# A unit's score maxima turned by VectorE's block transpose instead of a TensorE transpose, with sixteen row transfers in place of four

## The chip, the cores and the metric

The kernel runs on one core of one Trainium2 chip. Its time is the device time of one execution in microseconds (us); less is better.

## What is computed

The inputs are `x` (2048 x 640), attention weights `wqkv` and `wo` with 32 heads of 20 columns, four DFT matrices and a gate vector. Cut to what matters:

```python
def _A_ref(x, wqkv, wo):
    # q, k, v: 32 heads of 20 columns
    scores = jnp.einsum("bhqd,bhkd->bhqk", q, k) * (Dh ** -0.5)
    p = _softmax(scores, axis=-1)
    o = jnp.einsum("bhqk,bhkd->bhqd", p, v)
    return o @ wo
def _B_ref(x, ...):
    a, b = x @ dft_hid_re.T, x @ dft_hid_im.T
    return dft_seq_re @ a - dft_seq_im @ b
g = _sigmoid((x * gate_w).sum(-1, keepdims=True))
return g * a + (1 - g) * b
```

The softmax subtracts each query's maximum over all 2048 keys. That maximum, and the way it gets to where it is subtracted, is all that the change touches.

## The kernel before

**Units and the two score streams.** The attention is cut into 32 units (`NU`). A unit is a pair of heads (h = 0 on partitions 0 to 63, h = 1 on 64 to 127) and one half of the queries, 1024 of them. The scores are computed twice. In the first pass, "m" (`s_mm`, line 168), TensorE multiplies queries by keys with the queries on the partitions, and VectorE takes the maximum of each 128 x 512 block (line 170). In the second pass, "e" (in `score`, line 830), TensorE multiplies with the keys on the partitions and ScalarE takes the exponential (line 832). The exponential can't subtract a per-query number there, because the queries run along the free axis. So the subtraction is done in the matmul itself: `kst` has rows of ones and `qst` has two more rows per head, `KROWS` and `KROWS + 1`, which hold the negated maximum split in two parts (the second is what the first, rounded to fp32r, leaves over). The e matmul contracts over 62 rows, the m matmul over the first 60.

**How the maxima travel.** When a unit's 128 maxima tiles are done, `max_nm` (line 184) reduces them to a 128 x 16 tile of negated maxima: partition p and column 8h + q hold the query 128q + p of head h. `max_chain` (line 199) turns this by a TensorE transpose against an identity into a 16 x 128 tile in PSUM (line 202), and VectorE splits it into `m1` and `m2` (`split`, lines 112 and 113). Then SyncE copies, for each head and part, eight partitions of 128 numbers into one row of `qst` (lines 210 and 211): four transfers a unit, each in eight pieces of 512 bytes. An e matmul of the unit can start once they have landed.

**The order.** The body is one list of 256 cycles, written by hand; a unit takes eight of them:

```python
ORDER = "emFemFFFFemFeFFmeFFemFFFmmFFmeeB"
```

Each "e" and "m" is one score matmul, an "F" is a place where matmuls of the Fourier part are filled in (lines 346 and 575, later the output projection, line 646), and "B" is a burst: `max_nm` if a unit's maxima are complete, the reads of finished Fourier tiles (lines 354/355, 594/595, 655 to 658), the sixteen products of probabilities and values (`av_step`, line 494), and last `max_chain`. The m stream runs `LEAD` = 41 steps (a step is the two heads' scores of one block) ahead of the e stream. With these numbers, unit n's last m matmul stands in cycle 8n - 3, its `max_chain` at the end of that cycle's burst, and its first e matmul is the first of the two "e" at the end of cycle 8n - 1, two cycles later. `FIRST` makes that one the head h = 1. Unit 0 is handled in the prologue.

**Queues.** Every engine works through its own list in order. SyncE (SP) issues nearly all transfers: loads of DFT blocks (`raw<-in_cdft`, line 459), of operands kept in memory (`araw<-a_scr`, line 474), of partial sums (`yt<-y_scr`, line 567), of reciprocals of the softmax sums (`rb<-r_scr`, line 521), and stores (lines 679, 785). The four row transfers are put into SP's list at the second step after `max_chain`. The program gives SP's transfers eight completion semaphores in turn, so a transfer is issued only when the one eight places before it has landed. GpSimd (POOL) splits the loaded DFT blocks into two fp32r parts (lines 465, 479, 112, 113) for TensorE.

Five PSUM banks (`bank()`) go round between the score matmuls, and the transposed maxima take a turn there too.

Of the kernel before, what the change touches and what calls it, by code (L numbers as in the profile page):

```python
# [10 lines left out]
F32 = mybir.dt.float32  # L11
R = mybir.dt.float32r
AF = mybir.ActivationFunctionType
ALU = mybir.AluOpType
AX = mybir.AxisListType
# [3 lines left out]
P = 128  # L19
# [9 lines left out]
KROWS = 3 * DH  # L29
# [38 lines left out]
def f32(ap):  # L68
    return ap.bitcast(F32)
# [3 lines left out]
def mix_kernel(ctx: ExitStack, tc: tile.TileContext, xa, wqk, wb, cdft, wo, out):  # L73
    nc = tc.nc
    pe, act, dve, pool, sp = nc.tensor, nc.scalar, nc.vector, nc.gpsimd, nc.sync
    ctx.enter_context(tc.manual_schedule())

    def pools(**kw):
        return ctx.enter_context(tc.tile_pool(**kw))

    const = pools(name="const", bufs=1)
    small = pools(name="small", bufs=1)
# [14 lines left out]
    ident = const.tile([P, P], F32, name="ident")  # L97
# [10 lines left out]
    def split(dst1, dst2, src, e1, e2):  # L108
        if e1 is act:
            act.activation(dst1, src, AF.Copy)  # L110
        else:
            e1.tensor_copy(dst1, src)  # L112
        e2.tensor_tensor(dst2, src, f32(dst1), op=ALU.subtract)  # L113
# [8 lines left out]
    def bank():  # L122
        return ps_w.tile([P, 512], F32, name=f"ps{next(turn) % 5}")
# [23 lines left out]
    def q_unit(n):  # L147
        u = n % 2 * (S // 2)
        return qst[n // 2 % 2][:, u : u + S // 2]

    mx, nms, ends = {}, {}, []
    now, later = [-1], {}

    def at_step(i, fn):
        later.setdefault(i, []).append(fn)
# [16 lines left out]
    def s_end(i):  # L172
        n, s = divmod(i, 32)
        if n < NU and s == 31:
            if now[0] < 0:
                max_nm(n)
            else:
                ends.append(n)
        if s == 1 and 0 < n <= NU and now[0] < 0:
            max_chain(n - 1)  # L180

    def max_nm(n):
        nms[n] = small.tile([P, 16], F32, name="nm", bufs=2)
        dve.tensor_reduce(nms[n], mx.pop(n).rearrange("p h q c -> p (h q) c"), axis=AX.X, op=ALU.max, negate=True)

    def s_step(i):
        for fn in [s_mm(i, h) for h in range(2)]:
# [10 lines left out]

    def max_chain(n):
        q = q_unit(n)  # L200
        pt = bank()[:16, :P]
        pe.transpose(pt, nms.pop(n), ident)
        m1 = small.tile([16, P], R, name="m1")
        m2 = small.tile([16, P], R, name="m2")
        split(m1, m2, pt, dve, dve)

        def rows():
            for h in range(2):
                b = 64 * h + KROWS
                sp.dma_start(f32(q[b : b + 1, :]), f32(m1[8 * h : 8 * h + 8, :]))  # L210
                sp.dma_start(f32(q[b + 1 : b + 2, :]), f32(m2[8 * h : 8 * h + 8, :]))

        if now[0] < 0:
            rows()
        else:
            at_step(now[0] + 2, rows)
# [201 lines left out]
    for n, c in enumerate(order):  # L418
        for t in range(4):
            m = 4 * n + t  # L420
# [329 lines left out]
    for u in range(UNITS):  # L750
        k, t = LONG[u // HT], u % HT
# [14 lines left out]
    for k, tt in enumerate(PRE):  # L766
        i = 4 * (edge[-1] + 2 * k)
# [68 lines left out]
    def burst(c):  # L836
        for n in ends:
            max_nm(n)
        run_extras(max(done - HIDS, 0) // 3, 2)
        for kt in (2 * c, 2 * c + 1):  # L840
            av_step(now[0], kt // NS, kt % NS)
        while ends:
            max_chain(ends.pop(0))
        if c == HID - 1:
            start_dft()
# [135 lines left out]
```

## Time and profile before

| | |
|---|---|
| median of 3 runs | 1892.6 us (1891.74 to 1895.43) |
| span of the profiled execution | 1888.5 us |
| TensorE | 1877.4 us busy (99%) |
| VectorE | 1470.0 us (78%) |
| ScalarE | 1219.1 us (65%) |
| GpSimd | 1005.1 us (53%) |
| DMA engines | 280.50 MB, mean 149 GB/s |

The span goes from the first to the last instruction of one profiled execution; what lies around it is not in the page, and the median of the runs is 4.1 us above it. In the rows, PE is TensorE's matmuls, PEld its weight loads, DVE VectorE, ACT ScalarE and SPq the queue of SyncE. A row of the timeline gives the start and the duration in us, the engine, the line in the kernel, the operation, what it writes and reads, and in brackets how long the engine was idle before it and what ended that. A number after "x" counts instructions merged into the row.

### The profile page before, as it was taken

To read this page: it belongs to the slowest core of one execution; us is meant where nothing else is said; L and a number is where in the kernel's file an instruction comes from. 1 tells how busy PE (TensorE), PEld (TensorE's weight loads), DVE (VectorE), ACT (ScalarE), POOL (GpSimd) and SP (SyncE) were. 2 spreads that over 40 slices of the span, in tenths; PEclk is the share of its full clock that TensorE was granted. 3 is DMA by queue.
4 is the path that set the end of the run, shared out by engine and by line. 5 is a ranking of instruction groups with operands and counts; after the bars stand their busy time and mean duration, and the time that the engine had idled before them with its cause. 6 is when DMAs were issued, how large, how long until landed. Compare 5 with 4: busy or idle time off the path is not lost. (4 is left out here: it accounts for less than half of the span.)

```text
span 1888.5 us, 44537 instructions
## 1 busy us (share of the span) xinstructions
PE 1877.4 (99%) x17453; PEld 1358.2 (72%) x17453; DVE 1470.0 (78%) x2445; ACT 1219.1 (65%) x2350; POOL 1005.1 (53%) x872
## 2 busy tenths in 40 slices
PE   9999999999999999999999999999999999999998
PEld 8987777777776677776767677776767677766666
DVE  4145569989898888888888888888888888889954
ACT  4221147777777767666767667666767676677785
POOL 1200001010004999466699989958879988734343
PEclk9999999999999999999999999999999999999999
DMA  7843341221215575536557576736475746442214
GB/s 232 181 133 128 128 154 48 62 76 49 75 58 147 163 238 178 148 123 169 180 176 238 171 234 190 201 119 189 156 220 195 225 147 205 154 114 70 62 49 157
DMA packets 174804, 280.50 MB, mean 149 GB/s; under 512 B 44303, under 2 KB 106895, under 8 KB 174595
## 3 DMA queue, kind: packets, MB, share of 16 engines
q1 hardware_dynamic: 173635, 275.70, 47.7%
q0 software_dynamic: 960, 1.97, 0.6%
q8 instruction: 137, 2.24, 0.5%
q14 instruction: 72, 0.59, 0.1%
HBM read 213.37 MB, written 63.52 MB: 147 GB/s over the span
## 5 line engine op out<-in xcount | busy, mean ns | idle before, releaser
L170 DVE TENSOR_REDUCE mx<-ps 128x1 f32<-128x512 f32 x2048 | 1294.8, 684 | 175.8 <-PE ps L168 154.8
L832 ACT ACTIVATE p<-ps 128x512 f32<-128x512 f32 x2048 | 1087.0, 599 | 432.7 <-PE ps L168 223.6
L168 PE MATMUL ps<-kst,qst 60*128 60x512 f32 x2048 | 785.2, 415 | 3.7 <-DVE mx L170 1.7
L830 PE MATMUL ps<-qst,kst 62*128 62x512 f32 x2048 | 698.9, 413 | 0.5 <-ACT p L832 0.3
L575 PE MATMUL yp<-a,part 64*128 64x320 f32 x5376 | 649.1, 307 | 0.0
L575 PEld LDWEIGHTS yp<-a,part 64*128 64x128 f32 x5376 | 582.2, 186 | 7.3
L494 PE MATMUL av<-p,v 128*21 128x512 f32 x4096 | 491.3, 596 | 0.0
L830 PEld LDWEIGHTS ps<-qst,kst 62*128 62x128 f32 x2048 | 335.7, 185 | 200.9 <-DVE mx L170 182.4
L168 PEld LDWEIGHTS ps<-kst,qst 60*128 60x128 f32 x2048 | 371.2, 184 | 24.7 <-DVE mx L170 9.6
L113 POOL TENSOR_TENSOR part<-raw,part 128x1024 fp32r<-128x1024 f32 (+1 forms) x129 | 290.4, 2251 | 10.3
L494 PEld LDWEIGHTS av<-p,v 128*21 128x21 f32 x4096 | 98.4, 100 | 226.7 <-issue 223.2
L346 PE MATMUL yp<-wb,xs 64*128 64x320 f32 x1920 | 236.0, 308 | 0.1
L112 POOL CAST part<-raw 128x1024 fp32r<-128x1024 f32 (+1 forms) x129 | 127.0, 985 | 161.5 <-PE yp L575 141.2
L346 PEld LDWEIGHTS yp<-wb,xs 64*128 64x128 f32 x1920 | 206.0, 186 | 4.5 <-DVE raw L355 0.5
L465 POOL TENSOR_TENSOR raw<-raw,raw 128x1024 f32<-128x1024 f32 x77 | 185.4, 2408 | 6.4 <-DMA raw<-in_cdft 4.8
L112 POOL CAST wb<-raw 128x966 fp32r<-128x966 f32 (+1 forms) x4 | 3.4, 862 | 255.4 <-DMA raw<-in_wb 255.4
L524 POOL TENSOR_TENSOR o<-o,rb 128x512 f32<-128x512 f32 x31 | 40.2, 1296 | 146.6 <-DMA rb<-r_scr 100.8
L113 POOL TENSOR_TENSOR a<-araw,a 128x320 fp32r<-128x320 f32 x112 | 97.6, 872 | 9.0
L113 DVE TENSOR_TENSOR p<-ps,p 128x512 fp32r<-128x512 f32 x40 | 27.5, 691 | 93.5 <-ACT p L110 90.8
L646 PE MATMUL yp<-a,part 64*128 64x320 f32 x720 | 89.5, 309 | 0.0
L110 ACT ACTIVATE p<-ps 128x512 fp32r<-128x512 f32 x40 | 23.7, 597 | 100.6 <-PE ps L118 100.6
L646 PEld LDWEIGHTS yp<-a,part 64*128 64x128 f32 x720 | 76.9, 186 | 2.5
(86 smaller groups left out, 1237.0 us busy)
## 6 DMA issues: line engine op xcount, KB each, us to landing
raw<-in_cdft SPq DMA_DIRECT2D x192, 512.0 KB
araw<-a_scr SPq DMA_DIRECT2D x192, 160.0 KB
qk_scr<-p SPq DMA_DIRECT2D x40, 512.0 KB
kst<-qk_scr SPq DMA_DIRECT2D x90, 160.0 KB
qst<-qk_scr SPq DMA_DIRECT2D x90, 160.0 KB
a_scr<-raw SPq DMA_DIRECT2D x64, 160.0 KB
yt<-y_scr SPq DMA_DIRECT2D x64, 160.0 KB
y_scr<-yt SPq DMA_DIRECT2D x64, 160.0 KB
```

The source lines that it names most:

```text
L112: e1.tensor_copy(dst1, src)
L113: e2.tensor_tensor(dst2, src, f32(dst1), op=ALU.subtract)
L168: pe.matmul(ps, q[b : b + KROWS, qt * P : (qt + 1) * P], k[b : b + KROWS, kc * 512 : (kc + 1) * 512], start=True, stop=True)
L170: return lambda: dve.tensor_reduce(mx[n][:, h, qt, kc : kc + 1], ps, axis=AX.X, op=ALU.max)
L346: pe.matmul(yp[h][:, :HE], xs[r, xz, d, cs], w[r, wz, d, :HE], start=d == 0 and z == 0, stop=d == ND - 1 and z == 2)
L465: pool.tensor_tensor(raws[0], raws[0], raws[1], op=ALU.add if PRODUCTS[n][0][1][0] > 0 else ALU.subtract)
L494: pe.matmul(av[32 * j : 32 * j + DH + 1, :], v[:, kt, h * (DH + 1) : (h + 1) * (DH + 1)], pp[qc][:, h, :], start=kt == 0, stop=kt == NS - 1)
L524: pool.tensor_tensor(o, o, rb, op=ALU.mult)
L575: pe.matmul(yp[h][:, :HE], c[r, cz, cs], a[r, az], start=s == 0 and z == 0, stop=s == NS - 1 and z == 2)
L646: pe.matmul(yp[h][:, :HE], o[r, oz, d], wos[d, hf][r, wz], start=d == 0 and z == 0, stop=d == ND - 2 and z == 2)
L830: pe.matmul(pt, k[b : b + KROWS + 2, kt * P : (kt + 1) * P], q[b : b + KROWS + 2, qc * 512 : (qc + 1) * 512], start=True, stop=True)
L832: act.activation(pts[n, kt, qc][:, h], pt, AF.Exp, scale=float(DH) ** -0.5)
```

## The change

The negated maxima go into the first 16 columns of a 128 x 32 tile, one of two (`negs`) whose other columns are set to zero once at the start. VectorE's block transpose then turns each 32 x 32 block of it by itself, into PSUM: partition 32b + c, column j, gets the maximum of column c of partition 32b + j. The transposed tile is 128 x 32 in place of 16 x 128, and a row of `qst` is now collected from four groups of partitions. So VectorE splits 128 x 32 elements, and each of the four rows takes four transfers, one for each block b, of eight pieces of 128 bytes, laid down 512 bytes apart: sixteen transfers a unit. The TensorE transpose is gone. The places in the order of the work stay: `max_nm` and `max_chain` are called where they were, and the transfers are put into SP's list at the same step.

```diff
+    negs = [const.tile([P, 32], F32, name=f"neg{i}") for i in range(2)]
+    for t in negs:
+        pool.memset(t, 0.0)
...
     def max_nm(n):
-        nms[n] = small.tile([P, 16], F32, name="nm", bufs=2)
-        dve.tensor_reduce(nms[n], mx.pop(n).rearrange("p h q c -> p (h q) c"), axis=AX.X, op=ALU.max, negate=True)
+        nms[n] = negs[n % 2]
+        dve.tensor_reduce(nms[n][:, :16], mx.pop(n).rearrange("p h q c -> p (h q) c"), axis=AX.X, op=ALU.max, negate=True)
...
     def max_chain(n):
         q = q_unit(n)
-        pt = bank()[:16, :P]
-        pe.transpose(pt, nms.pop(n), ident)
-        m1 = small.tile([16, P], R, name="m1")
-        m2 = small.tile([16, P], R, name="m2")
-        split(m1, m2, pt, dve, dve)
+        pt = bank()[:, :32]
+        dve.transpose(pt, nms.pop(n))
+        ms = [small.tile([P, 32], R, name=f"m{z}") for z in range(2)]
+        split(ms[0], ms[1], pt, dve, dve)
 
         def rows():
             for h in range(2):
-                b = 64 * h + KROWS
-                sp.dma_start(f32(q[b : b + 1, :]), f32(m1[8 * h : 8 * h + 8, :]))
-                sp.dma_start(f32(q[b + 1 : b + 2, :]), f32(m2[8 * h : 8 * h + 8, :]))
+                for z, m in enumerate(ms):
+                    r = 64 * h + KROWS + z
+                    row = f32(q[r : r + 1, :]).rearrange("z (q b p) -> z b q p", q=8, b=4)
+                    for b in range(4):
+                        c = 32 * b + 8 * h
+                        sp.dma_start(row[:, b], f32(m[c : c + 8, :]))
```

## The prediction

> **What bounds the kernel now.** I read the page's head and its clock row first, then the busy times of one unit, then the timeline around one hand-over of a unit's maxima.
>
> ```profile
> span 1888.5 us, 44537 instructions
> PE 1877.4 (99%) x17453; PEld 1358.2 (72%) x17453; DVE 1470.0 (78%) x2445; ACT 1219.1 (65%) x2350; POOL 1005.1 (53%) x872
> PEclk9999999999999999999999999999999999999999
> ```
>
> TensorE is busy from end to end at a granted clock of 0.9 or more in all slices. A busy PE row can hide pipelining, so one unit is looked at by itself (columns: stretch, its length, busy us and instructions of PE, PEld, DVE, ACT, POOL, clock, DMA share, GB/s).
>
> ```profile
> 1011.00:1062.00 51.00, 51.00 (x519) 36.33 (x519) 42.94 (x72) 35.86 (x70) 49.21 (x41) 1.00 0.60 195
> ```
>
> VectorE is idle for 8 of 51 us and ScalarE for 15. TensorE sets the pace; what stops its list adds to the time, and what is taken from its list is gained. GpSimd, at 49.21, is the next in line, which a rival below takes up. Now the hand-over of unit 15 (three queries of the timeline):
>
> ```profile
> 1008.04 1.92 PE L494 MATMUL av<-p,v 128*21 128x512 f32 x16
> 1009.16 0.21 DVE L184 TENSOR_REDUCE nm<-mx 128x16 f32<-128x64 f32 x1
> 1009.88 0.28 PE L202 MATMUL ps<-ident,nm 128*16 128x128 f32 x1
> 1010.20 0.28 DVE L112 CAST m<-ps 16x128 fp32r<-16x128 f32 x1 [0.83 <-PE ps L202]
> 1010.51 0.28 DVE L113 TENSOR_TENSOR m<-ps,m 16x128 fp32r<-16x128 f32 x1
> ...
> 1010.51 0.68 SPq L210 DMA_DIRECT2D qst<-m  x1
> 1011.28 0.63 SPq L211 DMA_DIRECT2D qst<-m  x1
> 1011.97 0.64 SPq L210 DMA_DIRECT2D qst<-m  x1
> 1012.65 0.63 SPq L211 DMA_DIRECT2D qst<-m  x1
> 1013.33 0.91 SPq L459 DMA_DIRECT2D raw<-in_cdft  x2
> ...
> 1014.55 1.92 PE L494 MATMUL av<-p,v 128*21 128x512 f32 x16
> ...
> 1020.38 0.22 PEld L830 LDWEIGHTS ps<-qst,kst 62*128 62x128 f32 x2
> 1020.88 1.92 PE L494 MATMUL av<-p,v 128*21 128x512 f32 x16
> ```
>
> The reader is to see a chain with a deadline. The maxima are reduced at 1009.37, turned, split, and from 1010.51 on SyncE issues four row transfers, one every 0.69 us. The two L830 loads at 1020.38 are unit 15's first e matmuls, just ahead of a burst. From first issue to deadline there are 9.87 us, and the four issues take 2.77 of them. The present kernel has room here; the question is whether sixteen issues have it.
>
> **The transpose leaves TensorE.** The burst that ends with the transpose runs from 1008.04 to the next one at 1014.55, 6.51 us; the next cycle, without one, from there to 1020.88, 6.33 us. So a transpose costs TensorE about 0.2 us, and 31 of them (unit 0 is in the prologue) 6 us. This is the whole gain on the engine that sets the time, provided that nothing later in the unit takes it back.
>
> **VectorE's share.** No row shows a block transpose. The nearest small operations bound it:
>
> ```profile
> L184 DVE TENSOR_REDUCE nm<-mx 128x16 f32<-128x64 f32 x32 | 6.7, 210 | 0.1
> L438 DVE TENSOR_SCALAR ngate<-gate 128x16 f32<-128x16 f32 x1 | 0.2, 175 | 0.0
> L112 DVE CAST m<-ps 16x128 fp32r<-16x128 f32 x32 | 8.9, 279 | 14.4 <-PE ps L202 13.7
> ```
>
> It has 32 elements a partition, so 0.18 to 0.28 us; I take 0.21, as for the reduction of 64. The two split operations shrink from 128 elements a partition to 32, so each lies between 0.18 and 0.28; I take 0.18, near the 16-element row. Busy time is then 0.57 against 0.56 before: nothing, with 8 us of idle time a unit to cover any error. Its new waits, on the transfers of the unit before to have read the split tiles, are over some 40 us earlier, and the two memsets on GpSimd are needed only when unit 0 is complete, far into the prologue. But the chain is shorter, since VectorE no longer waits for TensorE's burst: reduction end at 1009.37, then 0.03 + 0.21 + 0.03 + 0.18 + 0.03 (gaps as between 1010.48 and 1010.51), first issue near 1009.9 in place of 1010.51. That is 0.6 us earlier. It holds only where VectorE does nothing else in between. The burst's reads of Fourier tiles come after the reduction and before the transpose:
>
> ```profile
> 402.89 0.49 DVE L355 TENSOR_TENSOR raw<-raw,yp 128x320 f32<-128x320 f32 x1
> 403.55 0.28 DVE L112 CAST m<-ps 16x128 fp32r<-16x128 f32 x1 [0.18 <-PE ps L202]
> ...
> 403.86 0.67 SPq L210 DMA_DIRECT2D qst<-m  x1
> ...
> 413.60 0.26 PEld L830 LDWEIGHTS ps<-qst,kst 62*128 62x128 f32 x2
> ```
>
> Here, in unit 3, the read ends at 403.38, transpose and copy would follow to about 403.85, and nothing is gained. Such a read stands in units 1 to 7, in one DFT unit of three (a Fourier tile ends every third cycle) and in units 29 and 30.
>
> **The sixteen transfers.** Twelve more issues a unit on SyncE. The new form, eight pieces of 128 bytes from SBUF to SBUF, is not in the trace. The rows that bound it (duration in ns, minimum/median/maximum):
>
> ```profile
> L210 SPq DMA_DIRECT2D qst<-m x64: 634/658/797, 228.7 to 1818.5; - x64
> L459 SPq DMA_DIRECT2D raw<-in_cdft x192: 328/376/1987, 561.3 to 1637.4; - x192
> L508 SPq DMA_DIRECT2D l_scr<-o x31: 527/542/555, 322.1 to 1826.8; - x31
> L916 SPq DMA_DIRECT2D raw<-o x4: 706/720/793, 1871.6 to 1874.0; - x4
> ```
>
> 128 pieces of 4 KB from memory take 0.33 us, four pieces of 2 KB to memory 0.54, eight pieces of 512 bytes inside SBUF 0.63, twenty of 2 KB inside SBUF 0.72. Bytes do not set the issue time: the largest transfer is the quickest. The new form has the old row's ends and its eight pieces, so I take its steady pitch of 0.685 us with the 0.05 gap, and for the range 0.59 (L508 with the gap) to 0.77 (L916). Sixteen then need 15 x 0.685 + 0.64 plus 0.1 for the two waits on VectorE, 11.0 us from first issue to last end, against 2.77. The eight semaphores in turn add nothing: the ninth issue comes 5.5 us after the first. How soon a row lands after its issue:
>
> ```profile
> GB/s 0 0 0 0 0 0 0 0 0 0 0 0 0 0 0 0 24 0 0 94 24 0 0 0 24 0 0 0 24 0 23 187 187 257 351 281 140 398 351 304
> ...
> 1871.61 3.09 SPq L916 DMA_DIRECT2D raw<-o  x4
> ...
> 1876.16 0.63 ACT L110 ACTIVATE part<-raw 128x512 fp32r<-128x512 f32 x1 [0.98 <-DMA raw<-o]
> ```
>
> In the first line 1009 to 1016 us are cut in 40 slices of 0.175 us; the four rows are the four 24s, the last at 1013.9 to 1014.1, 0.8 us after the last issue ended at 1013.28. In the tail, ScalarE gets 40 KB transfers inside SBUF 1.4 us after their last issue ended at 1874.70. I take 1.1, between them.
>
> The first e matmul is for h = 1, whose rows are the last eight of the sixteen, and it waits for all eight semaphores. So the rows are there 12.1 us after the first issue, and the deadline is 9.87 us after it, or 10.5 where the chain is shorter. TensorE stops with the fill matmuls, the burst of sixteen products and the next cycle queued behind. With these rows for the special units:
>
> ```profile
> 606.94 0.68 SPq L210 DMA_DIRECT2D qst<-m  x1
> 615.38 0.29 PEld L830 LDWEIGHTS ps<-qst,kst 62*128 62x128 f32 x2 [0.28 <-ACT p L832]
> 1817.00 0.68 SPq L210 DMA_DIRECT2D qst<-m  x1
> 1823.75 0.19 PEld L830 LDWEIGHTS ps<-qst,kst 62*128 62x128 f32 x2
> ```
>
> Lateness against the old e time: 14 DFT units without a read, 12.1 - 0.6 - 9.87 = 1.65, 23 us; 7 with one, 2.25, 16 us; units 1 to 6 (403.86 to 413.60 is 9.74) 2.4, 14 us; unit 7 (8.44) 3.7; units 29 and 30, estimated between these and the next, 2.7, 5; unit 31 (6.75, its chain two reads long, 0.9 shorter) 4.5. Together 66 us. The 0.2 us a unit that the transpose frees only makes TensorE arrive earlier and wait longer, so it is in this sum already, at zero. To restart, an e weight load, 0.19 us in the row above, has to run that was hidden behind matmuls: 31 x 0.2 = 6 us. What follows the rows in SP's list (L459 above, then operands, partial sums, reciprocals) goes out 8 us later; its consumer is GpSimd, which works ahead of TensorE:
>
> ```profile
> POOL part L112 <- PE yp L575: 141.2, 53, 7.4
> ```
>
> It waits 53 times for TensorE to free a buffer, and so has lead to lose; I count this at zero. Sum: 1888.5 + 66 + 6 = 1960.5 us of span, and with the 4.1 us by which the median of the runs exceeds the span, 1965 us.
>
> [...]
>
> **Rivals.**
>
> First, the sixteen rows still arrive in time: the issue is quicker for short pieces. The point is a pitch of (10.5 - 0.2 - 1.1 - 0.7) / 15 = 0.57 us. Then TensorE keeps the 0.2 us of each transpose: 1892.6 - 6 = 1886 us. For it: L459 shows that 0.33 is possible. Against it: both rows that go from SBUF to SBUF are above 0.63. Chance 0.10, faster.
>
> Second, it costs more. GpSimd has 49.21 of 51 us filled in the tightest units; when its loads come 8 us late in each, its lead of a few us runs out and TensorE waits for DFT parts too; if half of the 8 us came through in one unit of three, that is 10 x 4 = 40 us: 2005. Or the clock falls after each stop: if the next 3.4 us ran at half speed, 31 x 1.7 = 53 us, 2018. The rows show a full clock but also no stop of this length. [...] Chance 0.08 for both.
>
> Third, half of the stall is recovered, because ScalarE and VectorE empty their queues meanwhile and the next cycles run quicker: 1965 - 36 = 1929. Against it: the pace is TensorE's, and neither is awaited much. Chance 0.06.
>
> **How the numbers follow.** The forecast has 0.76. Pitch bounds move each unit by 15 x 0.1 = 1.5 us down, 46 in all, or 15 x 0.08 = 1.2 up, 37 in all: 1919 to 2002. That takes in the third rival and leaves out the first and most of the second. The chance of faster by over 0.2% (4 us, about what can be told from no change) is 0.10; within it 0.02, for a pitch near the point where the rows just arrive; slower 0.88.
>
> **What would show it.** In the changed profile: 512 row transfers of about 0.63 us; PEld L830 waiting for DMA `qst<-m` about 31 times for 2 us, as a new first line among the waits of TensorE; the L202 rows gone; cycles 8n - 1 near 8.5 us and the others unchanged. Wrong would be: row transfers below 0.57 us, no such wait, or cycles that lengthen elsewhere.

## The result, and the profile after

The changed kernel took 2019.5 us (median of four runs, 2016.2 to 2025.2) against 1892.2: 1.067 times as long, 95% interval [1.0659, 1.0685]. The prediction said slower, by less: 1965 us, 1919 to 2002. First the page of the changed kernel (span; busy time and share of TensorE), then its row for the granted clock:

```profile
span 2015.5 us, 45002 instructions
PE 1922.2 (95%) x17421; PEld 1366.3 (68%) x17421; DVE 1471.2 (73%) x2477; ACT 1222.1 (61%) x2350; POOL 1006.5 (50%) x874
```

```profile
core 0: 2015.5 us, clock 0.976
```

TensorE has 32 matmuls fewer and yet is busy for 45 us more, and the clock is no longer full: the same matmuls ran slower in places. In front of the first e matmul of a unit (L835) it stands idle for 72 us, in 31 stops (the waits; columns: total us, times, longest us):

```profile
PE ps L835 <- DMA qst<-m: 65.3, 28, 5.0
PE ps L835 <- issue: 6.8, 3, 2.9
```

The hand-over of unit 14, from three parts of the timeline (start us, us, engine, line, operation):

```profile
1015.52 1.92 PE L499 MATMUL av<-p,v 128*21 128x512 f32 x16
1016.68 0.21 DVE L187 TENSOR_REDUCE neg<-mx 128x16 f32<-128x64 f32 x1
1017.00 0.23 DVE L205 STREAM_TRANSPOSE ps<-neg 128x32 f32<-128x32 f32 x1
1017.26 0.19 DVE L112 CAST m<-ps 128x32 fp32r<-128x32 f32 x1
1017.48 11.28 SPq L216 DMA_DIRECT2D qst<-m  x16
1017.48 0.19 DVE L113 TENSOR_TENSOR m<-ps,m 128x32 fp32r<-128x32 f32 x1
...
1021.83 1.91 PE L499 MATMUL av<-p,v 128*21 128x512 f32 x16
...
1030.13 0.21 PEld L835 LDWEIGHTS ps<-qst,kst 62*128 62x128 f32 x2 [2.42 <-issue]
```

VectorE needs 0.8 us from the start of the reduction to the first issue (0.74 forecast); the burst's cycle is 6.31 us long, as forecast (both forecasts were worked out on unit 15, which like this one has no read of a Fourier tile); SyncE issues for 11.28 us, until 1028.76; and TensorE, which has nothing left from about 1028.0 on, starts again at 1030.13.

To find all of the 127 us, the starts of the bursts (L494 before, L499 after) are compared. They cut both traces into the same 255 cycles, eight to a unit, and the difference of each cycle is summed by its place in the unit. A cycle is named here by the burst that opens it, so the prediction's cycle 8n - 1, which ends with the burst behind the first e, is 8n - 2 here.

| cycles | after minus before, us | forecast |
|---|---|---|
| 8n - 3, with the transpose | -6.3 | -6, taken back by the stop |
| 8n - 2, to the late first e | +81.3 | 66 + 6, and the 6 |
| 8n - 1, right behind the stop | +44.4 | 0 |
| 8n - 5, pair changes and late loads | +7.1 | 0 |
| all else, prologue and tail included | +0.5 | 0 |

The first two lines are the forecast, 75 against 72 us. The miss is in the other two, above all in a cycle that has no stop of its own. What makes it longer is seen in two stops, by windows of 3.41 us (columns: window, its length, busy us and instructions of PE, PEld, DVE, ACT, POOL, granted clock, DMA share, GB/s). Units 11 and 14, in this order:

```profile
864.64:868.05 3.41, 1.65 (x18) 1.00 (x18) 2.32 (x4) 0.71 (x3) 0.38 (x1) 1.00 0.29 97
868.05:871.46 3.41, 3.41 (x18) 0.78 (x12) 0.00 (x0) 1.08 (x3) 0.00 (x0) 0.50 0.82 201
...
1025.07:1028.48 3.41, 2.91 (x34) 2.63 (x31) 3.36 (x6) 2.35 (x5) 3.26 (x5) 1.00 0.02 4
1028.48:1031.89 3.41, 1.73 (x15) 0.59 (x18) 0.90 (x2) 1.09 (x2) 0.00 (x0) 1.00 0.55 166
1031.89:1035.30 3.41, 3.41 (x40) 2.80 (x34) 2.28 (x4) 2.72 (x6) 0.94 (x1) 1.00 0.80 232
```

Unit 11's stop is the shorter one, 1.76 us, all in one window (3.41 - 1.65); the whole next window is at half clock, 18 matmuls in it. Unit 14's stop is longer, 0.50 + 1.68 us, but a window's edge cuts it, and the clock stays at 1.00, with 40 matmuls in the window after. In this trace's clock record there are 26 stretches at half clock, 98 us in all: 22 of 3.413 us, three of 6.827, and a last one of 2.769. Their starts (868.05, 922.66, 977.28 ...) are whole multiples of 3.413 us apart from the first to the last, and the windows above are cut by them. Of the windows of this trace at full clock, each of the 21 with at least 1.81 us of idle TensorE was followed by half clock; of the four with 1.73 to 1.78 us, three were; of the twelve with 1.07 to 1.68 us, one.

In 23 of the 31 cycles 8n - 1 some of the work runs at half clock: 82.8 us of busy TensorE, which at full clock would have taken about half, 41.4 us less (an estimate from these records). TensorE is idle there for only 4.3 us. Of the other eight, seven are at most 0.21 us longer than before, though the stops ahead of them were 1.55 to 2.68 us long; the eighth, unit 6, is 0.89 us longer, with an idle time of its own of 0.64 us.

### The profile page after: what moved, and what is told of

Read it like the earlier page. It is cut to its first block, busy times and chain, and to the rows that moved or that the text cites. A ratio compares the mean times of both kernels' runs of the same rounds, so it can differ in the third digit from the quotient of the medians.

```text
span 2015.5 us, 45002 instructions
## 1 busy us (share of the span) xinstructions
PE 1922.2 (95%) x17421; PEld 1366.3 (68%) x17421; DVE 1471.2 (73%) x2477; ACT 1222.1 (61%) x2350; POOL 1006.5 (50%) x874
## 5 line engine op out<-in xcount | busy, mean ns | idle before, releaser
L835 PE MATMUL ps<-qst,kst 62*128 62x512 f32 x2048 | 710.2, 422 | 72.6 <-DMA qst<-m 65.3
L580 PE MATMUL yp<-a,part 64*128 64x320 f32 x5376 | 650.3, 307 | 0.0
L580 PEld LDWEIGHTS yp<-a,part 64*128 64x128 f32 x5376 | 584.4, 187 | 8.2
L835 PEld LDWEIGHTS ps<-qst,kst 62*128 62x128 f32 x2048 | 338.7, 187 | 318.8 <-DVE mx L173 156.2
L499 PE MATMUL av<-p,v 128*21 128x512 f32 x4096 | 521.8, 628 | 0.0
L499 PEld LDWEIGHTS av<-p,v 128*21 128x21 f32 x4096 | 100.9, 102 | 239.9 <-issue 236.7
L351 PE MATMUL yp<-wb,xs 64*128 64x320 f32 x1920 | 240.6, 312 | 4.3 <-ACT raw L359 4.0
L351 PEld LDWEIGHTS yp<-wb,xs 64*128 64x128 f32 x1920 | 211.3, 189 | 10.0 <-ACT raw L359 4.9
```

Of the source, the lines that this page charges most:

```text
L351: pe.matmul(yp[h][:, :HE], xs[r, xz, d, cs], w[r, wz, d, :HE], start=d == 0 and z == 0, stop=d == ND - 1 and z == 2)
L499: pe.matmul(av[32 * j : 32 * j + DH + 1, :], v[:, kt, h * (DH + 1) : (h + 1) * (DH + 1)], pp[qc][:, h, :], start=kt == 0, stop=kt == NS - 1)
L580: pe.matmul(yp[h][:, :HE], c[r, cz, cs], a[r, az], start=s == 0 and z == 0, stop=s == NS - 1 and z == 2)
L835: pe.matmul(pt, k[b : b + KROWS + 2, kt * P : (kt + 1) * P], q[b : b + KROWS + 2, qc * 512 : (qc + 1) * 512], start=True, stop=True)
```

## The experiments

Three theories for the loss. A: SyncE's sixteen issues make the first e late, and a stop that leaves TensorE idle for more than half of a 3.41 us window is followed by half clock in the next, as in 24 of the 25 such windows above. B: VectorE's block transpose costs time. C: the slow cycle behind the stop is the refilling of empty queues. Ratios are to the kernel before, from runs on the same chip.

| kernel | median us | ratio, 95% interval | clock |
|---|---|---|---|
| before_16 | 2026.6 | 1.0709 [1.0693, 1.0725] | 0.975 |
| before_15 | 1993.3 | 1.0534 [1.0508, 1.0561] | 0.986 |
| before_14 | 1959.4 | 1.0367 [1.0331, 1.0402] | 0.995 |
| after_busy | 2007.7 | 1.0594 [1.0537, 1.0652] | 0.994 |
| after_busy12 | 2001.5 | 1.0576 [1.0558, 1.0593] | 0.994 |
| after_lead45 | 1939.8 | 1.0239 [1.0216, 1.0261] | 0.987 |
| before_lead45 | 1897.4 | 1.0021 [1.0011, 1.0030] | 0.998 |
| blocks | 1906.8 | 1.0070 [1.0055, 1.0085] | 0.997 |
| after_act | 2118.7 | 1.1202 [1.1187, 1.1216] | 0.949 |
| after_act_spread | 2032.3 | 1.0748 [1.0725, 1.0771] | 0.986 |
| after_act_lead45 | 2009.4 | 1.0632 [1.0617, 1.0647] | 0.982 |
| after_scr | 1887.4 | 0.9974 [0.9963, 0.9984] | 0.999 |

**The transfers alone.** TensorE's transpose stays; only the rows are cut into sixteen, fifteen or fourteen transfers.

```
     for z, m in enumerate((m1, m2)):
+        row = f32(q[r:r+1, :]).rearrange("z (q p) -> z q p", q=8)
+        for c0, c1 in itertools.pairwise(cuts[2 * h + z]):   # (0, 32, 64, 96, 128)
+            sp.dma_start(row[:, :, c0:c1], f32(m[8*h : 8*h+8, c0:c1]))
-        sp.dma_start(f32(q[r:r+1, :]), f32(m[8*h : 8*h+8, :]))
```

In before_15 the last row has three pieces, in before_14 two.

> The kernel before, with its TensorE transpose, but each of the four rows of a unit is moved in four transfers of eight 128-byte pieces, sixteen a unit, in the form that the change uses. Theory A (SyncE's issue of sixteen transfers makes the first e matmul late, and a stop of TensorE of over half a 3.4 us window is followed by a window at half clock): first issue to last landing 12 us as in the changed kernel, with the first issue some 0.6 us later in the 14 units without a read of a Fourier tile, so the changed kernel's time and up to 9 us more, 2015 to 2035 us. Theory B (VectorE's transpose or its place is what costs): the time of the kernel before, 1892 us.

> As the sixteen-transfer form of the kernel before, but one row goes in three transfers instead of four (two of 128-byte pieces, one of 256): fifteen a unit. Theory A: the last issue ends 0.69 us earlier, the stop is about 1.5 us in most units, under half of a 3.4 us window, so hardly a half-clock window in the clock record; 31 x 1.5 = 47 us and some 7 us of late loads: 1940 to 1955 us, some 75 us less than with sixteen. Theory C (the slow cycle after a stop is the refilling of empty queues and grows with any stop): the slow cycle shrinks only in proportion, 1.5 of 2.2, and the time is 1970 to 1985 us.

> As the sixteen-transfer form of the kernel before, but one row goes in two transfers: fourteen a unit. Theory A: the stop is about 0.8 us, no half-clock window; 31 x 0.8 = 25 us and some late loads: 1915 to 1930 us. Theory C: 0.8 of 2.2 of the slow cycle too, 1930 to 1945 us. If SyncE's issue is not the cause: 1892 us.

The wait of before_16, beside the 65.3 us of the changed kernel:

```profile
PE ps L833 <- DMA qst<-m: 70.0, 28, 5.7
```

Without any change on VectorE the whole loss is there, so B falls, and the loss belongs to the transfers. Fifteen and fourteen took longer than expected: their stop cycles are still 2.2 and 1.3 us longer each (68.4 and 39.7 us in sum, 87.5 with sixteen). Both totals lie above the ranges of theory A and of theory C, so they don't tell the two apart; the clock record does. The cycles behind the stop go with the stretches at half clock: 42.9, 21.5 and 12.9 us for 23, 13 and 6 of them in the whole trace. Cycles 8n - 5 gave 4 to 11 us in all three.

**The stop filled with work.** Ahead of a unit's first e, eight (after_busy) or twelve (after_busy12) matmuls whose result is overwritten keep TensorE busy while the rows are on their way.

```
     pt = bank()
+    if s == 0 and n > 0 and z == 0:
+        for _ in range(12):
+            pe.matmul(pt, k[b:b+KROWS, :P], q[b:b+KROWS, :512], start=True, stop=True)
```

> The changed kernel, with eight extra 60-row matmuls of 512 columns ahead of each unit's first e matmul, into the bank that this overwrites; they need no row transfer, so TensorE works about 1.7 us of the 2.2 us that it otherwise stops. Theory A: the rows land at the same time, but no window is idle for half of it, so the half-clock windows go and with them 44 us: 1968 to 1985 us, with a granted clock near 1.00. Theory C: the slow cycle after the stop stays or grows: 2015 us or more.

> The changed kernel with twelve throwaway 60-row matmuls ahead of a unit's first e instead of eight (2.6 us of cover at full clock, against a stop of 2.46). The stop becomes work, so no window of 3.4 us has 1.7 us of idle PE in it. Theory A (half clock comes from idle in the window before): the clock near 1.0, the cycle after the stall at its length of before (0 to 5 us over 31 units, against 44), the stall cycle 76 to 90, the time 1968 to 1990 and with little spread between runs. With eight the profiled run had 1988 and the runs 1990 to 2017: if that spread was half-clock windows that came or not by the phase of the window, it narrows here. If the cycle after the stall is long for another reason (queues that fill again), 2005 to 2020 again.

The cycle behind the stop went from 44.4 to 13.0 and 12.0 us, with the first e as late as before. With the seven cycles above, which followed a stop but no half clock and kept their length, this shows the half clock as the cause, and C falls. What is left is not spread over the units: in after_busy12 cycles 7, 23 and 47 hold 4.3, 6.8 and 1.3 us, in part half clock again, behind further stops. The total was above what I expected: 89.3 us in the stop cycles is the upper end of what I gave, these 12 us I had at 0 to 5, and 11.1 in cycles 8n - 5 not at all. With eight, the runs lay between 1990 and 2017 us. The fastest is the profiled one, with a mean granted clock of 0.994; the slower three had 0.989, 0.987 and 0.985, so they had more half clock. Which stops brought it is not known. In cycle 23 of the changed kernel itself the second cause can be read (timeline; in brackets the idle time before and what ended it):

```profile
424.71 1.31 SPq L216 DMA_DIRECT2D qst<-m  x2
426.07 0.91 SPq L283 DMA_DIRECT2D raw<-in_wb  x2
...
429.85 0.99 POOL L112 CAST wb<-raw 128x966 fp32r<-128x966 f32 x1 [53.43 <-DMA raw<-in_wb]
433.18 0.44 ACT L359 ACTIVATE raw<-yp 128x320 f32<-128x320 f32 x1 [4.46 <-POOL wb L113]
...
433.67 0.93 PE L351 MATMUL yp<-wb,xs 64*128 64x320 f32 x2 [2.11 <-ACT raw L359]
```

A weight load stands behind the sixteen rows on SyncE, so GpSimd splits it late and holds the raw buffer, ScalarE waits for that buffer, and TensorE for ScalarE. This stop of TensorE is a second one in the same unit, and half clock followed it as well (0.50 from 434.58 to 437.99).

**More lead.** `LEAD = 45` instead of 41 completes the maxima four steps earlier; before_lead45 is the control.

> The changed kernel with LEAD = 45 in place of 41: the m stream runs one cycle further ahead, so the rows' deadline is 6.3 us later and the sixteen transfers still have about 4 us to spare. Theory A: no stop at the first e matmul, no half-clock window, TensorE keeps 0.2 us for each transpose it no longer does: 6 us under the kernel before, to which comes what late loads cost GpSimd and so TensorE, 0 to 15 us (7 us of that stood outside the two slow cycles in the changed kernel): 1886 to 1901 us. Theory B: a time near the changed kernel's, 2000 us or more.

> The kernel before with LEAD = 45: the control for the longer lead. Its rows were in time already, so the lead should change nothing but a little more of the first scores without fill matmuls in the prologue and less at the end: 1890 to 1896 us on every theory.

The stop shrinks from 81.3 to 9.2 us and the cycle behind it from 44.4 to 0.6. But 39.1 us come up in cycles 8n - 5:

```profile
PE ps L171 <- DMA qst<-qk_scr: 21.2, 3, 10.5
PE ps L171 <- DMA o_scr<-o: 9.6, 2, 5.8
```

The m products of the next pair wait for operands whose loads stand in the same list (the profile puts two of these waits down to a store of `o`, also in that list). The control has 0.3 us in these cycles. The late list is thus a second way to lose time, and with more lead the larger one.

**Half of the issues on ScalarE.** First all eight rows of h = 1 in one piece (after_act), then two at each of the next four steps (after_act_spread), and these with a lead of 45.

```
-    sp.dma_start(row[:, b], f32(m[c : c + 8, :]))
+    (act if h else sp).dma_start(row[:, b], f32(m[c : c + 8, :]))       # after_act
+    at_step(now[0] + 3 + b, partial(act.dma_start, ...)) for h == 1     # spread
```

> The changed kernel, with the eight transfers of head h=1 issued from ScalarE's queue and the other eight from SyncE's, all at the same place as before. Theory A (the length of the list of issues on SyncE makes the first e late): each queue has 8 x 0.65 = 5.2 us and a landing of 1.02, so the rows are there 0.58 + 5.2 + 1.0 = 6.8 us after nm, against a need at some 9; the stop at the first e (81 us in the changed kernel) and the half clock after it (44) go to near zero, and the 6.5 us that TensorE saves shows: 1886 to 1893, if ScalarE's eight issues cost nothing. They stand ahead of exps in its queue, for 5.2 us in one piece: ScalarE's idle pieces in such a cycle are 1.3, 0.7, 0.9 and 2.7 us, so exps come up to 3 us late, banks come free late, and TensorE may stop for up to 3 us a unit: range 1886 to 1960, and the rows' own wait at L835 gone in either case. If the transfers themselves (sixteen of 128-byte pieces, whoever issues them) are the cost, the stop stays at some 2.4 us a unit: 2005 to 2025.

> The same, with ScalarE's eight issues spread: two at each of the four steps that follow the place of SyncE's eight. 2 x 0.65 us a step fits ScalarE's idle pieces of 0.7 to 2.7 us nearly. Theory A: no stop at the first e, no half clock, TensorE's 0.21 us a unit saved: 1884 to 1895, thus same or a little faster than before. If two issues a step push exps late all the same: up to 0.6 us at each of four steps, 31 units: up to 1960, with waits of PE ps on ACT in place of those on DMA. If late transfers of the rest of SyncE's list (8 issues, 5.2 us, against 4 of 0.7 us before) matter: 0 to 5 us at the pairs' changes.

> The spread version with a lead of 45 instead of 41. The changed kernel with lead 45 alone took 1940: its stop at the first e was gone, and 39 us had come at L171, in the m products that waited for the next pair's qst loads. If these were late because sixteen issues stood ahead of them in SyncE's list, eight make them less late by 8 x 0.685 = 5.5 us each, and most of the 39 go: 1890 to 1905 (the control, before with lead 45, took 1897). If lead 45 itself with the changed bank or buffer order makes the wait, it stays: 1925 to 1945.

SyncE's side came out as A has it: cycles 8n - 5 are at 0.0 us in the first two, and at -0.2 with a lead of 45, where they were at 39.1. The price on ScalarE was far above what I expected. Its waits, and TensorE's for it, in after_act:

```profile
ACT p L837 <- DMA qst<-m: 170.4, 31, 6.7
PE ps L835 <- ACT p L837: 151.8, 32, 6.1
```

An exp waits 5.5 us a unit for the eight issues ahead of it, and TensorE, which gets its banks back from the exps, for 4.9 of these. The trace has 32 stretches of half clock, of 220 us in all: 6.9 us each in the mean, against 3.8 (98 us in 26) in the changed kernel. I had given ScalarE's idle pieces as cover, but they lie between exps that TensorE needs at once. Spread, it still cost 23.1, 105.6 and 9.1 us in cycles 8n - 3, 8n - 2 and 8n - 1, and with a lead of 45, a cycle earlier, 26.5, 75.8 and 8.3 us. Not all of it is ScalarE's: of TensorE's waits in the spread version 41.1 us are for exps and 12.5 for transfers.

**Four transfers, VectorE's transpose.** Four 32x32 transposes set the blocks beside each other on the same partitions, so that the four row transfers of before serve.

```
+    pt = bank()[:32, :P]; nm = nms.pop(n)
+    for b in range(4):
+        dve.transpose(pt[:, 32*b : 32*b+32], nm[32*b : 32*b+32, :])
+    split(m1, m2, pt[:16, :], dve, dve)       # and the four transfers of before
```

> The changed kernel with VectorE's transpose in four pieces: each 32 x 32 block of its own is turned into the same 32 partitions of PSUM, at its own 32 columns, so the result is the 16 x 128 tile of the kernel before and four row transfers of 512-byte pieces do. Theory A: no stop, no late loads, and TensorE keeps the 0.2 us of 31 transposes: 1884 to 1888 us, under both kernels. Three more VectorE instructions of about 0.2 us a unit lie in its idle time and in the 6 us that the rows have to spare. Theory B: slower than before by the VectorE work if that is what costs, 1892 us or more.

The stop is gone (2.0 us), but cycles 8n - 3 are 13.0 us longer instead of 6 shorter. Unit 15:

```profile
1020.92 0.21 DVE L187 TENSOR_REDUCE neg<-mx 128x16 f32<-128x64 f32 x1
1021.23 0.97 DVE L207 STREAM_TRANSPOSE ps<-neg 32x32 f32<-32x32 f32 x4
1022.23 0.28 DVE L112 CAST m<-ps 16x128 fp32r<-16x128 f32 x1
1022.54 0.28 DVE L113 TENSOR_TENSOR m<-ps,m 16x128 fp32r<-16x128 f32 x1
1022.75 1.86 DVE L173 TENSOR_REDUCE mx<-ps 128x1 f32<-128x512 f32 x3
...
1023.48 0.18 PEld L835 LDWEIGHTS ps<-qst,kst 62*128 62x128 f32 x1 [0.29 <-DVE mx L173]
```

A 32x32 transpose takes 0.21 us, as long as one over 128 partitions in the changed kernel (0.22). The four keep VectorE from the reductions of the next products, and TensorE waits for a bank that one of them frees. VectorE's idle time elsewhere in the unit does not help here. This is read from one unit: over all cycles 8n - 3 TensorE's idle time is 5.5 us, and where the rest of the 19 us went is not shown.

**Few transfers by way of DRAM.** One VectorE transpose as in the change; four transfers write the blocks into a scratch in row order, two read them, two rows each, into `qst`.

```
+    def store():                                          # at step now + 2
+        for b in range(4):
+            dst = m_scr[n % 2, :, :, 32*b : 32*b+32].rearrange("z c p -> c z p")
+            sp.dma_start(dst, f32(ms[32*b : 32*b+16]))
+    def rows():                                           # at step now + 4
+        for h in range(2):
+            r = 64 * h + KROWS
+            sp.dma_start(f32(q[r:r+2, :]), m_scr[n%2, :, 8*h : 8*h+8, :].rearrange("z q c -> z (q c)"))
```

> The changed kernel's VectorE transpose and split, but the rows go through a scratch in DRAM: four transfers (16 partitions x 2 halves x 32 numbers each) write the blocks in the order of the rows, two transfers (two rows of 4 KB each) read them into qst. Six issues on SyncE in place of sixteen, with one wait for the writes between them. Theory A (what counts is the length of SyncE's list, not VectorE's transpose): issues 4 x 0.65 = 2.6 us from 0.58 after nm, the writes landed some 2 us later at 5.2, two reads issued by 6.5 and landed by 8 to 8.5, against a need at about 9; no stop or one of tenths of a us, the half clock gone, TensorE's 0.21 us x 31 = 6.5 us saved, SyncE's list 3 us a unit longer than before for the wait: 1884 to 1895. If the way through DRAM takes 1 us more than that, a stop of 0.5 us a unit: 1900 to 1905, still without half clock (below 1.7 us of idle). If theory B had a part after all (VectorE's transposing and splitting 32 columns of 128 partitions), it would show as a longer cycle 8n-3 and a time of 1895 to 1910 without stops at L216's rows.

Its hand-over of unit 15:

```profile
1008.62 1.92 PE L503 MATMUL av<-p,v 128*21 128x512 f32 x16
1009.76 0.21 DVE L188 TENSOR_REDUCE neg<-mx 128x16 f32<-128x64 f32 x1
1010.07 0.23 DVE L206 STREAM_TRANSPOSE ps<-neg 128x32 f32<-128x32 f32 x1
...
1010.78 1.73 SPq L213 DMA_DIRECT2D m_scr<-m  x4
...
1014.10 0.57 SPq L218 DMA_DIRECT2D qst<-m_scr  x2
...
1014.93 1.91 PE L503 MATMUL av<-p,v 128*21 128x512 f32 x16
...
1020.74 0.21 PEld L839 LDWEIGHTS ps<-qst,kst 62*128 62x128 f32 x2
```

The last issue ends at 1014.67, six us ahead of the first e. Cycles 8n - 3 are 6.1 us shorter in sum, all others are within 0.5 us of before, and the prologue is 3.0 us longer. The ratio is 0.9974 [0.9963, 0.9984]: a little faster than both kernels.

## Why the prediction was right and wrong

Right, by its own steps:

- TensorE's saving of 0.2 us a unit: 6.3 us in the 31 cycles with the transpose.
- VectorE: 0.21 us for the transpose and 0.18 for each split operation were taken; the groups of the changed kernel say (busy us, mean ns)

```profile
L205 DVE STREAM_TRANSPOSE ps<-neg 128x32 f32<-128x32 f32 x32 | 7.1, 222 | 1.5
L112 DVE CAST m<-ps 128x32 fp32r<-128x32 f32 x32 | 6.1, 191 | 1.1
```

- The issue, taken from the old row transfers: 634 ns was the smallest and 635 the median, and sixteen took 11.28 us in unit 14 and 10.94 in unit 11, where 11.0 was forecast (duration in ns, minimum/median/maximum):

```profile
L216 SPq DMA_DIRECT2D qst<-m x512: 634/635/1476, 229.4 to 1945.7; - x171
```

- The landing: TensorE started 1.37 and 1.34 us after the last issue ended in these two units, for 1.1.
- Lateness of 66 and restart of 6 us: 81.3 - 6.3 = 75. Unit by unit it fits too: with the 0.2 us by which TensorE arrives earlier, the sum gives stops of 3.9 us in unit 7 and 4.7 in unit 31, and 3.7 and 5.0 were measured.

The prediction calls 0.33 and 0.63 us the issue times of L459 and L210; these are the smallest in their rows, and the medians are 0.38 and 0.66. Its sum does not go by them.

Wrong were two terms that stood at zero. The first is the clock. The second rival had a price for it, 53 us and 2018, but only 0.08 of the chance, shared with another case, and the forecast's sum and its range had nothing for it. No row of the kernel before shows the 3.4 us at half speed in that price; the changed kernel's clock record has 3.413 us in 22 of its 26 stretches. The runs showed at least 32 us (44.4 less the 12.0 that are left with TensorE kept busy), and the trace about 41, as estimated above. The step that failed was to hold a stop of 2 us too short to halve the clock: that was the author's estimate, and no row showed it. In the changed kernel's trace 1.81 us of idle in one window was always enough, and 23 of the 31 units had half clock behind their stop.

The second is what follows the rows in SyncE's list, counted at zero because GpSimd works ahead. GpSimd's lead did hold in the tight DFT units, so that the 40 us of the rival did not come: TensorE has no wait at these units' DFT matmuls (L580) among its waits. But not everything in the list is GpSimd's. It carries the sums of the softmax, read back as `lc`, on which a reciprocal on VectorE waits: 5.7 us in four waits, and none before. In unit 17, at the largest of them (timeline):

```profile
1274.49 0.34 SPq L516 DMA_DIRECT2D lc<-l_scr  x1
1279.96 0.25 DVE L519 RECIPROCAL lc<-lc 128x16 f32<-128x16 f32 x1 [2.93 <-DMA lc<-l_scr]
1280.81 0.59 PE L171 MATMUL ps<-kst,qst 60*128 60x512 f32 x1 [2.69 <-DVE mx L173]
```

The load is issued 1.2 us behind the burst that opens this cycle, where it was 5.2 ahead of it in the kernel before; the reductions behind the reciprocal free their banks late, and TensorE stops. Three such stops make nearly all of the 7.1 us in cycles 8n - 5. In the early units the list also holds up a `raw` buffer that ScalarE needs, in units 1 and 6 by the store of a Fourier tile (`a_scr<-raw`), in unit 3 by the weights (`in_wb`) as shown above: 4.3 us of idle TensorE behind the stops of these three. The operands of a pair, also in the list, were waited for only with the longer lead.

Together: 1888.5 + 75.0 + 44.4 + 7.1 + 0.5 = 2015.5. The first rival's point, a pitch of 0.57 us, was not reached with the new form; its result, 1886, is what after_scr gave (1887.4) with transfers that are quicker to issue. The third rival, half of the stall recovered, had no sign in any cycle.

## What to carry to other kernels

Where TensorE sets the time, a stop had two prices here: its length, and the half clock behind it, by estimate 1.7 us for each 3.413 us of it, which followed 24 of the 25 windows with 1.73 us or more of idle TensorE in the changed kernel; so price every new stop of that length with both. A longer list of issues delayed what was queued behind it (the `lc` load of unit 17 by 6.4 us), so walk the whole list and ask of each entry who waits for it. Few transfers with a detour beat many direct ones here (1887.4 against 2019.5 us). Before issues move to another engine, see whether its next instruction is awaited at once: ScalarE's was, and eight issues ahead of it cost TensorE 4.9 us a unit.

## What was not expected of the hardware

How short an idle time half clock followed: 1.81 us in one window of 3.413 was always enough in the changed kernel's trace, and of the 16 windows with 1.07 to 1.78 us four were followed by it. So idle time alone does not decide the cases between, and what else does is not shown.

And the time to issue a small transfer did not go with its size. Inside SBUF its median was 0.64 us for pieces of 128 bytes (L216, above) and 0.66 for pieces of 512 (L210 of the kernel before); for the detour (same columns as above)

```profile
L213 SPq DMA_DIRECT2D m_scr<-m x128: 319/416/1524, 230.5 to 1815.1; - x128
...
L218 SPq DMA_DIRECT2D qst<-m_scr x64: 223/254/455, 233.3 to 1816.9; - x64
```

it was 0.42 us to DRAM and 0.25 from it, so six transfers took 2.3 us of issue in unit 15 where sixteen took 11.28 in unit 14 of the changed kernel. The number and shape of the pieces differ as well, and no run changed the direction alone.
